# Sums from transposed quarters, shorter runs of sums on GpSimd, and moments by twos in a fused attention and SwiGLU kernel

## The chip, the cores and the metric

The kernel runs on one core of a Trainium2 chip. The metric is device time in microseconds (us) of one execution; the time of a kernel is the median of its runs. The engines are called as the profile calls them: PE is TensorE (matmuls, transposes), ACT is ScalarE, DVE is VectorE, POOL is GpSimd, and SP is SyncE, which here only issues transfers. An engine works through its own queue in order; a transfer that POOL issues stands in POOL's queue between its sums.

## The reference

The input x has 2048 rows of 1024 values. Its rows are normalised, and the result goes through two branches whose outputs are combined:

```python
xn = _layernorm(x)                          # (x - mean) / sqrt(var + 1e-5), by row
# A: linear attention, 32 heads of 32
qkv = xn @ wqkv                             # 1024 -> 3 x 1024
phi = lambda t: where(t > 0, t + 1, exp(t)) + 1e-6
kv  = einsum("bhsd,bhse->bhde", phi(k), v)  # summed over all 2048 rows
z   = phi(k) summed over the rows
s   = (phi(q) @ kv) / (phi(q) . z + 1e-6) @ wo
# B: SwiGLU with 3584 hidden columns
out = (silu(xn @ w1) * (xn @ w3)) @ w2
return x + s * silu(out)
```

All values are float32.

## The kernel before

**Arithmetic.** Every large product is cut into two by two blocks and done with seven block products instead of eight (the Winograd form of Strassen's method). On the left it needs the quarters A11, A12, A22 of the rows and four sums of quarters:

S1 = A21 + A22, S2 = S1 - A11, S3 = A11 - A21, S4 = A12 - S2.

The right-hand side has its own four sums, T1 to T4. Each operand is split (`split`, L79) into a rounded high part, which ACT writes (L83), and the rest, which DVE writes (L84); a block product takes three matmuls for each slice of 128 (`mm3`, L89 to L94).

**Halves.** The rows are taken in two halves of 1024 (`half`, L426), each as two chunks of 512. A half needs its seven operands (`AOPS`) transposed, with the 1024 columns of x on the partitions: 128 partitions, high and low part, 4 slices, 512 rows. With these it makes keys and values, then queries, then the gate and up products (`gemm`, L310: keys and values of 4 pairs, queries of 4 pairs, gate and up of 14 pairs). The second stage, attention and the down product (`Segment`, L715), follows the two halves.

**First half's operands.** `prepare_first` (L158) loads four tiles of 128 rows, takes each one's mean and 1/sqrt(variance) (`moments`, L124), normalises it (L145), and turns A11 and A12 with four PE transposes each (L152). `prepare_rest` (L171) does the same for the four tiles of the second chunk, makes S1 to S4 on POOL (`combined`, L183, lines 186 to 189) from row tiles, and turns five operands. The order of these pieces among the first products is written out by hand at L450.

**Second half's operands.** `prepare_next` (L192) makes them while the first half's queries and first gate and up products run. Each of its four jobs loads two row tiles, takes moments of both, normalises them, makes the four sums on POOL with `combined`, turns seven operands (`turn`, L195; transposes at L198), splits each out of PSUM, and stores it in device memory (`a_d`, L201), from where the second half loads it.

**Fillers.** A job is a Python generator. `catch_up` (L298) is called six times in each product of `gemm` and takes the next step of the first job waiting; `issue_after` keeps the step's instructions behind the marks given. In the first half the jobs are the four of `prepare_next`, then 28 of `weight_sums` (L545), which load a piece of w2, make T1 to T4 on POOL (`sums_of`, L538, lines 540 to 543) and store them. In the second half they are `denominators` (L603), `merge_wo` (L657, which calls `sums_of` too) and `divide` (L631, which calls `four_sums`).

**Hidden tiles.** `hidden` (L514) takes a gate product through Silu on ACT into a tile `sg`, multiplies it by the up product on DVE (L524), stores it from POOL's queue (L525), and, once two tiles of a chunk are there, makes S1 to S4 on POOL (`four_sums`, L503, lines 509 to 512) into two tiles `hs`, which SP's queue stores (L534; POOL's for the last pair). `sg` has four buffers.

**Order.** The program is written in Python order. A planner (`schedule_with_timeline_sim`) then fixes each engine's order from its own estimates of when things are ready, and the order of the operations in the profile isn't always that of the text: sums of different steps stand side by side in POOL's queue. [...]

Of the kernel before, what the change touches and what calls it, by code (L numbers as in the profile page):

```python
# [9 lines left out]
F32 = mybir.dt.float32  # L10
# [12 lines left out]
def tile_linear_attention_times_swiglu(  # L23
# [100 lines left out]
    def moments(xs, dst):  # L124

        n = len(xs)
        bs = st.tile([P, n, 2, nc.vector.BN_STATS_DIM], F32, tag="bs", name="bs")
        v = st.tile([P, n], F32, tag="v", name="v")
        u = st.tile([P, n], F32, tag="u", name="u")
# [4 lines left out]
        y = dst[:, :, 1]  # L134
        nc.vector.tensor_scalar_add(v, y, 1e-5)
# [4 lines left out]
        nc.vector.tensor_mul(u, u, v)  # L140
        nc.vector.tensor_scalar(u, u, -0.5, 1.5, op0=ALU.mult, op1=ALU.add)
        nc.vector.tensor_mul(y, y, u)
# [27 lines left out]

    def prepare_rest(A, mom, i, t0):  # L171

        t1 = job_tile([P, D], f"xb{i}") if i < 3 else pb.tile([P, D], F32, tag="b", name=f"xb{i}")
        nc.sync.dma_start(out=t1, in_=x[C + i * P:C + (i + 1) * P, :])
        j = TH // 2 + i
        moments([t1], mom[:, j:j + 1])
        normalise(t1, mom[:, j])
# [14 lines left out]
    def prepare_next(i):  # L192


        def turn(n, src):  # L195
            p_ = bank(f"t{n}1_{i}")
            for k in range(ND // 2):
                nc.tensor.transpose(p_[:, k * P:(k + 1) * P], src[:, k * P:(k + 1) * P], ident)  # L198
            o = pb.tile([P, 2, ND // 2, P], FR, tag="b", name=f"{n}o{i}")
            split(o, p_.rearrange("p (k s) -> p k s", k=ND // 2))  # L200
            nc.sync.dma_start(out=a_d[n][:, :, :, i * P:(i + 1) * P], in_=o.bitcast(F32))  # L201

        def steps(_):
            t0, t1, t2 = (job_tile([P, D], f"xn{i}_{e}") for e in range(3))
            for c, t in enumerate((t0, t1)):
                r0 = HS + c * C + i * P
                nc.sync.dma_start(out=t, in_=x[r0:r0 + P, :])
# [3 lines left out]
            moments([t0, t1], m)  # L211
            yield True
            yield True
            normalise(t0, m[:, 0])
            yield True
            normalise(t1, m[:, 1])
# [731 lines left out]
```

## Time and profile before

| | us |
|---|---|
| median of 3 runs | 2450.59 (2450.36 to 2451.07) |
| the profiled execution | 2447.93 |
| its span, first to last instruction | 2446.1 |
| PE busy | 2358.0 (96%) |
| DVE busy | 1792.1 (73%) |
| ACT busy | 919.8 (38%) |
| POOL busy | 724.4 (30%) |
| mean granted clock of PE | 0.992 |

Busy time is the time in which an engine has an instruction under way, and this includes the time in which an instruction under way is held up by something else. A row of a timeline gives start and duration in us, engine, line, operation, the tile written and the tiles read, their shapes, and how many equal instructions it stands for. A row of a wait gives who waited for whom, the total, how often, and the longest. The stages lie about so in the span: the first half's operands until 64 us, its keys and values to about 200, its queries to about 320, its gate and up products to about 890, the second half to about 1740, then attention's output and the down product.

### The profile page before, as it was taken

Reading aid. Unit: us, or ns where it says so; the run is one execution under the profiler, and the core shown is the slowest. Engines: PE = TensorE matmul, PEld = TensorE weight load, DVE = VectorE, ACT = ScalarE, POOL = GpSimd, SP = SyncE. Lnnn points to the kernel's source line nnn. Section 1 sums busy time; section 2 is a strip of 40 time slices with the busy share of each in tenths; the row PEclk is TensorE's granted clock in tenths of the full one; section 3 lists DMA queues with packets and bytes.
Section 4 is the critical chain, followed back from the end, with each engine's and each line's share of the span. In section 5 each row is a group of like instructions: output and inputs, shape, how many; then the busy total and the mean of one; then the engine's idle time right before and its main releaser. Section 6 shows DMA issues by size and latency. Waiting matters only on the chain.

```text
span 2446.1 us, 31065 instructions
## 1 busy us (share of the span) xinstructions
PE 2358.0 (96%) x10624; PEld 1941.1 (79%) x10624; DVE 1792.1 (73%) x2694; ACT 919.8 (38%) x1648; POOL 724.4 (30%) x873
## 2 busy tenths in 40 slices
PE   5999998999999999999999999999999999999998
PEld 4788887778888888888888888888787788787876
DVE  7654777797777765558878878887745776767798
ACT  4333543323333234445433233323423434343443
POOL 3000122264545310001235552354210032323244
PEclk9999999999999999999999999999999999999999
DMA  3112455575656491124355664566755554454588
GB/s 129 52 52 69 140 170 162 157 257 181 207 173 219 149 345 52 35 78 153 128 196 200 218 227 151 183 230 216 241 157 178 149 156 143 134 153 127 161 277 266
DMA packets 377423, 408.12 MB, mean 167 GB/s; under 512 B 19824, under 2 KB 307568, under 8 KB 377264
## 3 DMA queue, kind: packets, MB, share of 16 engines
q1 hardware_dynamic: 355248, 332.46, 43.2%
q0 software_dynamic: 22016, 73.68, 8.0%
q8 instruction: 83, 1.36, 0.2%
q14 instruction: 76, 0.62, 0.1%
HBM read 268.44 MB, written 137.63 MB: 166 GB/s over the span
## 4 chain that ended last, share of the span: by engine, by line
PE 79%; DVE 11%; issue 4%; DMA 4%; ACT 2%; POOL 1%; SPq 0%; DVEq 0%; ACTq 0%; POOLq 0%
PE dB L92 1%; PE dB L94 1%; PE cB L92 1%; PE dB L93 1%; PE cB L94 1%; PE cB L93 1%; PE kv L415 1%; PE aB L94 1%; PE aB L92 1%; PE aB L93 1%; DMA wpr<-wp_d 1%; DVE acc L865 1%; PE trk L382 1%; DMA rT2B<-wt_d 1%; DMA rA11B<-h_d 1%
## 5 line engine op out<-in xcount | busy, mean ns | idle before, releaser
L474 POOL DMA_DIRECT2D pq_d<-pq x32 | 17.5, 547 | 502.0 <-DVE pq L376 501.9
L525 POOL DMA_DIRECT2D h_d<-sg x112 | 61.5, 549 | 278.5 <-DVE sg L524 257.8
L792 POOL TENSOR_TENSOR acc<-acc,uB 128x512 f32<-128x512 f32 x25 | 41.9, 1676 | 158.4 <-DVE uB L790 158.4
L540 POOL TENSOR_TENSOR w<-w 128x256 f32<-128x256 f32 x28 | 27.8, 992 | 103.5 <-DMA w<-in_B_w 103.5
L509 POOL TENSOR_TENSOR qd<-qd 128x128 f32<-128x128 f32 x32 | 26.6, 832 | 104.2 <-DVE qd L650 100.6
L512 POOL TENSOR_TENSOR hs<-sg,hs 128x256 f32<-128x256 f32 x56 | 54.9, 981 | 2.1
L771 POOL TENSOR_TENSOR acc<-acc,uB 128x512 f32<-128x512 f32 x7 | 11.7, 1666 | 145.8 <-ACT uB L763 145.8
L856 POOL DMA_DIRECT2D s_d<-s x32 | 17.3, 540 | 122.5 <-DVE s L798 64.5
L383 ACT ACTIVATE kvr<-trk 128x512 f32<-128x512 f32 x32 | 19.1, 597 | 77.7 <-PE trk L382 77.5
L510 POOL TENSOR_TENSOR hs<-hs,sg 128x256 f32<-128x256 f32 x56 | 45.9, 820 | 0.0
L511 POOL TENSOR_TENSOR hs<-sg 128x256 f32<-128x256 f32 x56 | 42.8, 765 | 0.0
L509 POOL TENSOR_TENSOR hs<-sg,sg 128x256 f32<-128x256 f32 x56 | 42.0, 749 | 1.1
L92 PE MATMUL cB<-T,XA22B 128*128 128x512 f32 x87 | 35.0, 403 | 6.6 <-DVE acc L796 6.2
L794 POOL TENSOR_TENSOR acc<-acc,uB 128x512 f32<-128x512 f32 x25 | 40.1, 1604 | 0.0
L83 ACT CAST XS4B<-rS4B 128x384 fp32r<-128x384 f32 (+1 forms) x40 | 19.6, 490 | 53.2 <-PE cB L94 45.2
L807 DVE TENSOR_TENSOR acc<-cB,acc 128x512 f32<-128x512 f32 x25 | 17.2, 688 | 30.2 <-PE cB L94 30.2
L84 DVE TENSOR_TENSOR XS1B<-rS1B,XS1B 128x384 fp32r<-128x384 f32 (+1 forms) x40 | 37.2, 931 | 1.7 <-ACT XS1B L83 1.6
L863 ACT ACTIVATE acc<-acc 128x512 f32<-128x512 f32 x32 | 20.2, 632 | 47.2 <-DVE acc L798 14.1
L83 ACT CAST XA11B<-rA11B 128x384 fp32r<-128x384 f32 (+1 forms) x40 | 19.7, 493 | 45.8 <-PE dB L94 28.4
L83 ACT CAST XS1B<-rS1B 128x384 fp32r<-128x384 f32 (+1 forms) x40 | 19.7, 493 | 45.4 <-PE cB L94 26.5
L83 ACT CAST XS3B<-rS3B 128x384 fp32r<-128x384 f32 (+1 forms) x40 | 19.6, 491 | 43.7 <-PE bB L94 15.6
L92 PE MATMUL aB<-B,XA12B 128*128 128x512 f32 x87 | 34.1, 392 | 1.9 <-ACT uB L788 1.6
(5864 smaller groups left out, 8907.8 us busy)
## 6 DMA issues: line engine op xcount, KB each, us to landing
h_d<-sg POOLq DMA_DIRECT2D x112, 256.0 KB, 4.4
hs_d<-hs SPq DMA_DIRECT2D x104, 256.0 KB
qs_d<-qd POOLq DMA_DIRECT2D x32, 512.0 KB, 4.4
w<-in_B_w SPq DMA_DIRECT2D x56, 256.0 KB
wt_d<-w SPq DMA_DIRECT2D x28, 512.0 KB
pq_d<-pq POOLq DMA_DIRECT2D x32, 256.0 KB, 3.0
pqd<-pq_d SPq DMA_DIRECT2D x16, 512.0 KB
S<-a_dS SPq DMA_DIRECT2D x16, 512.0 KB
```

What stands on the lines that cost most here:

```text
L83: nc.scalar.copy(out=hi, in_=src)
L84: nc.vector.tensor_sub(out=lo, in0=src, in1=hi.bitcast(F32))
L92: nc.tensor.matmul(acc, lhsT=wh, rhs=ah, start=start, stop=False, skip_group_check=True)
L93: nc.tensor.matmul(acc, lhsT=wh, rhs=al, start=False, stop=False, skip_group_check=True)
L94: nc.tensor.matmul(acc, lhsT=wl, rhs=ah, start=False, stop=stop, skip_group_check=True)
L509: nc.gpsimd.tensor_add(out=s1, in0=a21, in1=a22)
L510: nc.gpsimd.tensor_sub(out=s2, in0=s1, in1=a11)
L511: nc.gpsimd.tensor_sub(out=s3, in0=a11, in1=a21)
L512: nc.gpsimd.tensor_sub(out=s4, in0=a12, in1=s2)
L525: nc.gpsimd.dma_start(out=h_d[i][2 * h + c][:, 2 * k + n], in_=sg[n, c])
L792: G.tensor_add(out=c22, in0=c22, in1=u)
L794: G.tensor_add(out=c12, in0=c12, in1=u)
```

## The change

**`moments`** takes up to two tiles at once, and its last steps are fused: u = -0.5 y y v in one operation, and (u + 1.5) y in another, instead of a product, a scale and shift, and a product. `prepare_first` calls it for two tiles together, where it called it tile by tile. A new `load_second` loads the second chunk's tiles by twos and takes their moments together; `prepare_rest` calls it for tiles 0 and 2.

**`prepare_next`** turns the four quarters A11, A12, A21, A22 instead of the seven operands. A11 and A12 are split and stored out of PSUM as before, and ACT copies them, and A21, from PSUM over the row tile's own quarter. A22 is split and stored out of PSUM. The sums are then made on DVE, in place, from the transposed quarters, and split from there. It uses two job tiles instead of three.

**Runs of sums on POOL.** `four_sums` now yields after S1 and S2 and after S3 and S4; in `hidden` a store stands at each yield, and all these stores are issued from POOL's queue. `sums_of` yields, that is, ends a step, between its two pairs of sums; `weight_sums` begins its sums one step earlier, and `merge_wo` has one step more in each second job. `divide` runs through `four_sums` without anything between.

```diff
     def moments(xs, dst):
         n = len(xs)
-        bs = st.tile([P, n, 2, nc.vector.BN_STATS_DIM], F32, tag="bs", name="bs")
-        v = st.tile([P, n], F32, tag="v", name="v")
-        u = st.tile([P, n], F32, tag="u", name="u")
+        bs = st.tile([P, 2, 2, nc.vector.BN_STATS_DIM], F32, tag="bs", name="bs")
+        v, y, u = (st.tile([P, 2], F32, tag=a, name=a)[:, :n] for a in "vyu")
...
-        y = dst[:, :, 1]
-        nc.vector.tensor_scalar_add(v, y, 1e-5)
+        nc.vector.tensor_scalar_add(v, dst[:, :, 1], 1e-5)
         nc.scalar.activation(y, v, AF.Sqrt)
         nc.vector.reciprocal(y, y)
         nc.vector.tensor_mul(u, y, y)
-        nc.vector.tensor_mul(u, u, v)
-        nc.vector.tensor_scalar(u, u, -0.5, 1.5, op0=ALU.mult, op1=ALU.add)
-        nc.vector.tensor_mul(y, y, u)
+        nc.vector.scalar_tensor_tensor(u, u, -0.5, v, op0=ALU.mult, op1=ALU.mult)
+        nc.vector.scalar_tensor_tensor(dst[:, :, 1], u, 1.5, y, op0=ALU.add, op1=ALU.mult)
@@ prepare_first
-            for e in range(2):
-                i = 2 * g + e
-                xs.append(t[:, e])
-                moments(xs[i:], mom[:, i:i + 1])
+            xs += [t[:, e] for e in range(2)]
+            moments(xs[2 * g:], mom[:, 2 * g:2 * g + 2])
+            for i in (2 * g, 2 * g + 1):
                 normalise(xs[i], mom[:, i])
@@ prepare_rest
+    def load_second(mom, g):
+        ts = []
+        for i in (2 * g, 2 * g + 1):
+            ts.append(job_tile([P, D], f"xb{i}") if i < 3 else pb.tile([P, D], F32, tag="b", name=f"xb{i}"))
+            nc.sync.dma_start(out=ts[-1], in_=x[C + i * P:C + (i + 1) * P, :])
+        j = TH // 2 + 2 * g
+        moments(ts, mom[:, j:j + 2])
+        return ts
...
+        if i % 2 == 0:
+            seconds += load_second(mom, i // 2)
@@ prepare_next
+            return p_
+        def keep(n, src):
             o = pb.tile([P, 2, ND // 2, P], FR, tag="b", name=f"{n}o{i}")
-            split(o, p_.rearrange("p (k s) -> p k s", k=ND // 2))
+            split(o, src.rearrange("p (k s) -> p k s", k=ND // 2))
             nc.sync.dma_start(out=a_d[n][:, :, :, i * P:(i + 1) * P], in_=o.bitcast(F32))
...
-            turn("A11", t0[:, :C])
-            yield True
-            turn("A12", t0[:, C:])
-            yield True
-            b = combined(t0, t1, t2[:, :C])
-            yield True
-            for n in ("A22", "S1", "S3", "S2", "S4"):
-                yield True
-                turn(n, b[n])
+            for n, a in (("A11", a11), ("A12", a12)):
+                p_ = turn(n, a)
+                keep(n, p_)
+                nc.scalar.copy(out=a, in_=p_)
+                yield True
+            p_ = turn("A21", a21)
+            nc.scalar.copy(out=a21, in_=p_)
+            yield True
+            p_ = turn("A22", a22)
+            keep("A22", p_)
+            nc.vector.tensor_add(out=a22, in0=p_, in1=a21)
+            yield True
+            nc.vector.tensor_sub(out=a21, in0=a11, in1=a21)
+            keep("S1", a22)
+            yield True
+            keep("S3", a21)
+            nc.vector.tensor_sub(out=a11, in0=a22, in1=a11)
+            yield True
+            keep("S2", a11)
+            nc.vector.tensor_sub(out=a12, in0=a12, in1=a11)
+            yield True
+            keep("S4", a12)
             yield True
@@ four_sums
         nc.gpsimd.tensor_sub(out=s2, in0=s1, in1=a11)
+        yield
         nc.gpsimd.tensor_sub(out=s3, in0=a11, in1=a21)
         nc.gpsimd.tensor_sub(out=s4, in0=a12, in1=s2)
+        yield
@@ hidden, sums
-            four_sums(sg[0, c], sg[1, c], *o)
-            for e in range(2):
-                queue = nc.gpsimd if pair == NF // 2 - 1 else nc.sync
-                queue.dma_start(out=hs_d[i][2 * h + c][:, k, e], in_=o[e])
+            for e, _ in enumerate(four_sums(sg[0, c], sg[1, c], *o)):
+                nc.gpsimd.dma_start(out=hs_d[i][2 * h + c][:, k, e], in_=o[e])
@@ sums_of
         nc.gpsimd.tensor_sub(out=b12, in0=b22, in1=b12)
+        yield True
         nc.gpsimd.tensor_sub(out=b22, in0=b22, in1=b11)
@@ weight_sums
             yield True
-            yield True
-            sums_of(*(t[:, i] for i in range(4)))
+            yield from sums_of(*(t[:, i] for i in range(4)))
             yield True
@@ divide
-            four_sums(t[:, 0], t[:, 1], t[:, 2], t[:, 3])
+            for _ in four_sums(t[:, 0], t[:, 1], t[:, 2], t[:, 3]):
+                pass
@@ merge_wo
-                sums_of(*b)
+                yield from sums_of(*b)
```

More of the change, by code (lines that the diff above doesn't have):

```diff
@@ L169, in prepare_first, with prepare_rest @@
         return xs
[L171 to L177, printed above, removed]
+    def load_second(mom, g):
[6 more added lines that the diff above has]
+        return ts
+    def prepare_rest(A, mom, i, t0, seconds):
+        if i % 2 == 0:
+            seconds += load_second(mom, i // 2)
+        t1 = seconds[i]
+        normalise(t1, mom[:, TH // 2 + i])
         b = combined(t0, t1, small(f"S1x{i}"))
@@ L198, in turn @@
                 nc.tensor.transpose(p_[:, k * P:(k + 1) * P], src[:, k * P:(k + 1) * P], ident)
+            return p_
+        def keep(n, src):
             o = pb.tile([P, 2, ND // 2, P], FR, tag="b", name=f"{n}o{i}")
-            split(o, p_.rearrange("p (k s) -> p k s", k=ND // 2))
+            split(o, src.rearrange("p (k s) -> p k s", k=ND // 2))
             nc.sync.dma_start(out=a_d[n][:, :, :, i * P:(i + 1) * P], in_=o.bitcast(F32))
         def steps(_):
-            t0, t1, t2 = (job_tile([P, D], f"xn{i}_{e}") for e in range(3))
-            for c, t in enumerate((t0, t1)):
+            t = [job_tile([P, D], f"xn{i}_{e}") for e in range(2)]
+            for c in range(2):
                 r0 = HS + c * C + i * P
-                nc.sync.dma_start(out=t, in_=x[r0:r0 + P, :])
+                nc.sync.dma_start(out=t[c], in_=x[r0:r0 + P, :])
             for _ in range(3):
@@ L445, in half @@
             mom = st.tile([P, TH, 2], F32, tag="mom", bufs=1, name="mom")
-            xs = prepare_first(A, mom)
+            xs, seconds = prepare_first(A, mom), []
             m = [keys(0, early=True), values(0, early=True), keys(1, early=True)]
-            r = [prepare_rest(A, mom, i, xs[i]) for i in range(TH // 2)]
+            r = [prepare_rest(A, mom, i, xs[i], seconds) for i in range(TH // 2)]
             for kind, i in zip("mrrrmmrmrmrmrr", (0, 0, 1, 2, 1, 0, 3, 2, 0, 1, 1, 2, 2, 3)):
```

7 lines of the change are left out of this document (4 added, 3 removed).

## The prediction

> **What bounds the kernel now.** I read the page's head first, then the table of stretches, then who TensorE (PE) waited for, then the timeline around each of its longest waits.
>
> ```profile
> PE 2358.0 (96%) x10624; PEld 1941.1 (79%) x10624; DVE 1792.1 (73%) x2694; ACT 919.8 (38%) x1648; POOL 724.4 (30%) x873
> ```
>
> PE is the bound, idle for 4% of the span. So a change can gain in two ways: fewer PE instructions, or fewer of those idle stretches (and of the half-speed clock behind them). The stretches (columns: length, then PE, PEld, DVE, ACT, POOL busy, clock, DMA share, GB/s) say where they lie:
>
> ```profile
> 279.00:560.00 281.00, 263.60 (x1176) 214.52 (x1175) 221.05 (x306) 105.56 (x182) 98.95 (x120) 0.97 0.59 185
> 600.00:800.00 200.00, 200.00 (x884) 165.67 (x883) 153.65 (x190) 62.45 (x105) 102.62 (x124) 1.00 0.58 196
> ```
>
> From 600 to 800 us PE is never idle: nothing that VectorE (DVE) or GpSimd (POOL) saves there can count. From 279 to 560 us, where the second half's operands are prepared, PE is idle for 281 - 263.6 = 17.4 us and its clock is at 0.97, another 281 x 0.03 = 8.4 us. Its waits (us in total, times, longest), at the start and from 380 to 520 us:
>
> ```profile
> PE tA L152 <- DVE xa L145: 21.8, 3, 12.3
> PE bk__696 L92 <- ACT T2k__682 L83: 8.0, 1, 8.0
> ```
>
> ```profile
> PE ag__4061 L94 <- DVE B21g__4050 L84: 5.2, 1, 5.2
> PE ag__3357 L94 <- DVE B11g__3331 L84: 3.8, 1, 3.8
> PE bg__3380 L92 <- ACT T2g__3339 L83: 2.7, 1, 2.7
> PE bu__3890 L92 <- ACT T2u__3854 L83: 1.8, 1, 1.8
> ```
>
> 29.8 us are the start; 5.2 + 3.8 + 2.7 + 1.8 = 13.5 us are four waits for weight splits. The timeline (start, duration) shows why two of them were late:
>
> ```profile
> 396.78 4.88 DVE L84 TENSOR_TENSOR B11g__3331<-wg__3329,B11g__3331 128x512 fp32r<-128x512 f32 x1
> ...
> 500.42 10.28 DVE L84 TENSOR_TENSOR B21g__4050<-wg__4033,B21g__4050 128x512 fp32r<-128x512 f32 x1
> ```
>
> ```profile
> 399.18 1.25 POOL L189 TENSOR_TENSOR xn<-xn 128x512 f32<-128x512 f32 x1
> 400.40 0.71 POOL L512 TENSOR_TENSOR hs<-sg,hs 128x256 f32<-128x256 f32 x1
> ...
> 508.75 1.39 POOL L543 TENSOR_TENSOR w<-w 128x256 f32<-128x256 f32 x2
> ```
>
> Below, such an operation takes 0.68 us. Here it ends about 0.6 us after the last sum of an unbroken POOL run: at 401.7 after a run that ends at 401.1, at 510.7 after one that ends at 510.1. So while POOL sums run back to back, a DVE operation on two SBUF tiles is held to the end of the run. DVE runs in order, so each later split is late too.
>
> **The change, part by part.** The sum is made against the profiled execution, 2447.93 us (1.8 us around its span); the median of the runs is 2450.59, which is 2.66 more.
>
> *Transposes.* Each of four preparations turns four 128x512 quarters instead of seven operands: 12 turns, 48 transposes, go.
>
> ```profile
> 413.65 0.39 PE L94 MATMUL dg__3382<-S,T1g__3335 128*128 128x512 f32 x1
> 413.88 0.60 PE L198 MATMUL tA<-ident,xn 128*128 128x128 f32 x4
> 414.31 0.27 PE L198 MATMUL tS<-ident,xn 128*128 128x128 f32 x1
> 414.34 0.47 PE L94 MATMUL bg__3380<-S,T2g__3339 128*128 128x512 f32 x1
> 414.65 0.39 PE L92 MATMUL bg__3380<-S,T2g__3339 128*128 128x512 f32 x1
> ```
>
> Five transposes took 414.34 - 413.88 = 0.46 us, 0.092 each; the matmul behind them took 0.31 to its successor instead of 0.23. A turn thus costs 4 x 0.092 + 0.08 = 0.45 us on the bounding engine. 12 x 0.45 = **-5.4 us** (-4.4 without the switch, -6.5 if it is paid on both sides).
>
> *Preparing the second half.* The sixteen POOL sums go; DVE gets sixteen, ACT twelve copies of turned quarters out of PSUM.
>
> ```profile
> L189 POOL TENSOR_TENSOR xn<-xn x4: 1250/1295/1687, 283.8 to 467.2; 128x512 f32<-128x512 f32 x4
> ...
> L83 ACT CAST S4o<-tS x4: 580/587/599, 306.6 to 501.6; 128x512 fp32r<-128x512 f32 x4
> L84 DVE TENSOR_TENSOR S4o<-tS,S4o x4: 678/680/681, 307.7 to 511.8; 128x512 fp32r<-128x512 f32 x4
> ```
>
> The columns are ns: least, median, most. POOL loses 16 x 1.3 = 21 us of runs, DVE gains 16 x 0.68 = 11 us, ACT 12 x 0.59 = 7 us. ACT is busy 105.56 of 281 us and hides its part. DVE is busy 221.05 of 281, part of it being held. Against the change stands that S4o above, read from PSUM, was never held, while its successor reads two SBUF tiles: 16 splits and 12 of the sums become liable to be held. What falls away: POOL's runs shrink here by the L189 kind, and what stays (hidden sums, weight sums) is cut into twos by a store or a step. How much a cut helps shows at 1731 us, where a store of sums already stands between sums:
>
> ```profile
> 1730.50 3.28 DVE L84 TENSOR_TENSOR wp<-wpr,wp 128x512 fp32r<-128x512 f32 x2
> ```
>
> ```profile
> 1732.12 0.73 POOL L511 TENSOR_TENSOR hs<-sg 128x256 f32<-128x256 f32 x1
> 1732.79 0.56 POOL L534 DMA_DIRECT2D hs_d<-hs  x1
> 1733.37 1.00 POOL L510 TENSOR_TENSOR hs<-hs,sg 128x256 f32<-128x256 f32 x1
> ```
>
> The first of the two DVE operations takes its 0.6, so the held one gets about 2.7 us, ends at 1733.78 and has been let in at the store, although two more sums follow. A hold of 2.7 instead of 4.9 to 10.3 us is nearer to the 600 to 800 us stretch, where PE doesn't wait at all. Best case: all 13.5 us of those waits and 8 us of clock behind them go, -21.5. Worst: none goes and the new DVE work lies wholly on the path, +11. The row nearest to the case is the cut run, so I take -21.5 and give back 4.5 for the 28 operations newly liable and the sums that wait, in DVE's order, for a turn on PE: **-17 us**. Next late is what makes up the other 17.4 - 13.5 = 3.9 us, which stays.
>
> [...]
>
> *Moments by twos.* At the start six small operations for each tile become five for two tiles, and the chain from statistics to normalise loses one link.
>
> ```profile
> 20.61 0.20 DVE L141 TENSOR_SCALAR u<-u 128x1 f32<-128x1 f32 x2
> ...
> 23.23 0.21 DVE L142 TENSOR_TENSOR mom<-mom,u 128x1 f32<-128x1 f32 x2
> ```
>
> Between links lie 23.23 - 20.61 = 2.6 us of other DVE work, and PE's first waits are for the normalise at the chain's end. One link less: **-2.4 us**. If another link is also overtaken less, -5; if the first tile's normalise waits for the second's statistics with nothing regained, +3. The second four tiles, loaded by twos, have PE's products as cover, which begin with this row:
>
> ```profile
> 29.19 0.79 PE L92 MATMUL ak__341<-A,B11k__334 128*128 128x512 f32 x1
> ```
>
> *Stores on POOL's queue, steps.* 104 stores of hidden sums leave SP's queue.
>
> ```profile
> L534 SPq DMA_DIRECT2D hs_d<-hs x104: 319/336/2637, 360.7 to 1691.0; - x104
> ...
> L534 POOL DMA_DIRECT2D hs_d<-hs x8: 539/557/559, 884.9 to 1736.0; - x8
> ```
>
> POOL pays 104 x 0.557 = 58 us, at 30% busy over the whole span; behind a store only the next pair of sums waits. SP stops waiting for sums ahead of weight fetches. The weight sums come a step earlier, so POOL may wait longer for their load, with stores of sg tiles behind it:
>
> ```profile
>   ACT sg L521: 9.2, 4
> ```
>
> ACT waited 9.2 us behind such sums and PE not at all. **0**, from -1 to +6 (two thirds of that wait reaching PE).
>
> [...]
>
> *Second half of the run.* Where wo is merged, PE waits as well:
>
> ```profile
> PE cg__9630 L92 <- DVE c22g__9657 L344: 1.4, 1, 1.4
> PE wp L92 <- ACT kvm L83: 1.4, 1, 1.4
> ```
>
> The merged sums are cut too, one step longer in each of four jobs. I take **-2** (-2.8, or +2 if the longer jobs crowd the end).
>
> Sum: -5.4 - 17 - 2.4 + 0 - 2 = -26.8. 2447.93 - 26.8 = 2421.1 for a profiled execution, 2423.8 on the median: **2424 us**.
>
> **The rivals.**
>
> *Holds replaced by other waits.* The planner may still line up sums of different steps (the run that ends at 401.1 us already mixes an xn sum with hidden sums), and the new DVE sums come in ahead of weight splits. For it: DVE is busy 0.79 of this stretch; against it: stores now stand between the sums. Then the transposes, the start and a third of -21.5 remain against a few us of new waits: 2450.6 - 5.4 - 2.4 - 7 + 4 = 2440. This is also what follows if breaking the runs doesn't do what it says.
>
> *One instruction at a time.* If a held operation waits for a single sum, runs don't matter and cutting gains nothing: only the 1.25 us that L189 put into one wait, the 1.8 us wait behind its longest row (1687 ns), 8.4 / 4 = 2.1 us of clock behind that one, transposes and start: 2450.6 - 3.05 - 2.1 - 5.4 - 2.4 = 2438. Against it: the 10.28 row. [...]
>
> *Slower.* DVE now waits in order for a chain PE, ACT, DVE in each preparation. ACT waited for such turns before:
>
> ```profile
>   ACT A22o L83: 11.4, 3
> ```
>
> That is 3.8 us each. Eight such waits (A21 and A22 of four preparations) would be 30 us of DVE standing before weight splits. Its place is DVE's queue, and it decides once a wait comes between a split and the product that needs it within about a microsecond, as at 397 us. With half of it on PE and 2.1 us of clock behind each of four, 15 + 8 us, and the old waits unmended: 2450.6 + 23 - 7.8 = 2466. Against it: the planner put ACT's and DVE's work on S1o to S4o behind the same kind of turns without a wait of PE of that size.
>
> **How the numbers follow.** Forecast 0.62 (its own range 2411 to 2437, from the terms' ends taken partly together); replaced waits 0.19; one at a time 0.05; slower 0.09; no change, small terms of both signs, 0.05. A difference under 0.2% (4.9 us) can't be told from none here. Faster: 0.62 + 0.19 + 0.05 less a little of the second, 0.84; same 0.06; slower 0.10. The range leaves out the last two and reaches over the first rivals: 2411 to 2445.
>
> **What would show it.** 48 fewer instructions of PE; no POOL sum of xn after 100 us; the first product before 29 us; from 280 to 560 us DVE operations of at most 3 us and PE idle for under 9 us at a clock of 0.99. The forecast is wrong if PE's idle time there stays near 17 us, or if new waits of more than 3 us for DVE's sums or ACT's copies appear.

## The result, and the profile after

The changed kernel takes **2516.23 us** (2508.32 to 2518.87), against 2450.48 for the kernel before beside it: a ratio of **1.0264, 95% interval 1.0239 to 1.0289**. It is 65 us slower, where 27 us faster was forecast; the time lies far outside the range, and the forecast's rival on the slower side (2466) doesn't reach it either. The profiled execution took 2518.11 us.

The head of the page after, and the group that stands out in its list (busy time and mean, then the idle time of the engine just before the group, and what ended it):

```profile
span 2516.3 us, 30839 instructions
...
PE 2379.0 (95%) x10576; PEld 1950.9 (78%) x10576; DVE 1805.1 (72%) x2678; ACT 925.9 (37%) x1656; POOL 761.0 (30%) x961
...
L673 DVE SCALAR_TENSOR_TENSOR qd<-qd 128x512 f32<-128x512 f32 x32 | 23.1, 721 | 87.0 <-DMA qd<-pq_d 87.0
```

PE has 48 instructions fewer and is nevertheless busy for 21 us longer, and its idle time has grown as well. The group below it belongs to a part of the kernel that the change hardly touches: L673 is the VectorE product in `divide` (L650 before, where `divide` begins at L633; lines behind `prepare_next` are 23 to 25 higher than before). DVE stood 87 us in front of it, for its loads. In the kernel before, the same group has 0.0 us of idle time in front of it (21.8 us busy, 682 ns each).

The stretches say where the time went (columns as in the prediction). Before:

```profile
1300.00:1800.00 500.00, 495.92 (x2174) 406.98 (x2173) 397.47 (x519) 170.99 (x292) 212.40 (x316) 1.00 0.62 206
```

After:

```profile
279.00:560.00 281.00, 262.30 (x1158) 212.75 (x1157) 229.02 (x328) 117.12 (x199) 97.07 (x130) 0.98 0.60 193
1300.00:1800.00 500.00, 450.22 (x1881) 363.71 (x1880) 358.60 (x456) 146.76 (x253) 223.67 (x336) 0.95 0.53 177
```

In the last stretch PE is idle 495.92 - 450.22 = 45.7 us more, and its clock falls from 1.00 to 0.95, another 500 x 0.05 = 25 us. Added, these are about 71 us, an estimate, since the clock is given to two places; the two profiled executions lie 70.2 us apart, so the loss lies in this stretch in the main. The stretch from 279 to 560 us, on which the forecast rested, has stayed as it was: PE idle for 281 - 262.30 = 18.7 us (17.4 before), clock 0.98 (0.97 before). Who waited, in the whole run (total, times, longest):

```profile
DVE qd L673 <- DMA qd<-pq_d: 87.0, 16, 8.3
PE cg__12885 L92 <- DVE c22g__12917 L367: 9.1, 1, 9.1
PE bg__2990 L92 <- ACT T2g__2954 L83: 6.1, 1, 6.1
PE cg__13211 L92 <- DVE c22g__13243 L367: 5.9, 1, 5.9
PE cg__11221 L92 <- DVE c22g__11253 L367: 5.4, 1, 5.4
PE ak__321 L93 <- DVE A L84: 4.0, 1, 4.0
```

Three of the PE waits are one kind: PE adds its next block product to PSUM bank c, and L367, which has to read the bank first, is late. From 1300 to 1800 us such waits for L367 make up 37.7 us. The timeline around a smaller one shows why (start, duration; the bracket is the idle time before):

```profile
PE cu__11050 L92 <- DVE c22u__11082 L367: 3.2, 1, 3.2
```

```profile
1387.04 0.69 DVE L673 SCALAR_TENSOR_TENSOR qd<-qd 128x512 f32<-128x512 f32 x1 [6.86 <-DMA qd<-pq_d]
1391.18 0.68 DVE L673 SCALAR_TENSOR_TENSOR qd<-qd 128x512 f32<-128x512 f32 x1
...
1396.18 0.57 POOL L676 DMA_DIRECT2D qs_d<-qd  x1 [0.30 <-POOL qd L536]
...
1400.72 0.38 SPq L261 DMA_DIRECT2D wu__11172<-in_B_w  x1
1401.21 0.54 SPq L665 DMA_DIRECT2D qd<-r_d  x1
...
1403.89 1.94 SPq L667 DMA_DIRECT2D qd<-pq_d  x1
...
1412.23 0.69 DVE L673 SCALAR_TENSOR_TENSOR qd<-qd 128x512 f32<-128x512 f32 x1 [7.57 <-DMA qd<-pq_d]
1412.84 0.68 DVE L367 TENSOR_TENSOR c22u__11082<-cu__11050,uu__11028 128x512 f32<-128x512 f32 x1
...
1438.01 0.69 DVE L673 SCALAR_TENSOR_TENSOR qd<-qd 128x512 f32<-128x512 f32 x1 [7.23 <-DMA qd<-pq_d]
```

DVE stands for 7.57 us in front of a division, and L367, the sum that reads the bank, stands right behind it: PE's last matmul into the bank ahead of that sum ran from 1404.33 to 1404.72, and L367 began at 1412.84, 0.61 us after the division. ACT and POOL show the same order of work in the kernel before: ACT stood 2.48 us, until 500.53, for a weight piece, with the S4 that it copied at 501.58 turned by 496.05; POOL stood 1.37 us, until 489.24, for a load, with the hidden tiles that it stored from 489.92 on done by 487.23.

So the question was: why are the loads of a division late now, when the work of `divide` and its loads are as before?

### The profile page after: what moved, and what is told of

The parts are those of the page before. It is cut to its first block, busy times and chain, and to the rows that moved or that the text cites. A ratio compares the mean times of both kernels' runs of the same rounds, so it can differ in the third digit from the quotient of the medians.

```text
span 2516.3 us, 30839 instructions
## 1 busy us (share of the span) xinstructions
PE 2379.0 (95%) x10576; PEld 1950.9 (78%) x10576; DVE 1805.1 (72%) x2678; ACT 925.9 (37%) x1656; POOL 761.0 (30%) x961
## 4 chain that ended last, share of the span: by engine, by line
PE 54%; DMA 11%; DVE 7%; issue 4%; POOL 2%; SPq 2%; ACT 1%; DVEq 0%; POOLq 0%; ACTq 0%
DMA qd<-pq_d 4%; DMA qs_d<-qd 2%; PE dB L92 1%; PE dB L94 1%; PE dB L93 1%; PE cB L92 1%; PE cB L94 1%; PE cB L93 1%; PE aB L94 1%; PE aB L92 1%; PE aB L93 1%; SPq L665 1%; DMA wpr<-wp_d 1%; SPq L667 1%; DMA rS1B<-hs_d 1%
## 5 line engine op out<-in xcount | busy, mean ns | idle before, releaser
L497 POOL DMA_DIRECT2D pq_d<-pq x32 | 17.4, 545 | 520.4 <-DVE pq L399 498.4
L673 DVE SCALAR_TENSOR_TENSOR qd<-qd 128x512 f32<-128x512 f32 x32 | 23.1, 721 | 87.0 <-DMA qd<-pq_d 87.0
L557 POOL DMA_DIRECT2D hs_d<-hs x112 | 62.0, 554 | 5.9 <-POOL hs L536 3.3
L563 POOL TENSOR_TENSOR w<-w 128x256 f32<-128x256 f32 x28 | 25.8, 922 | 94.9 <-DMA w<-in_B_w 94.8
L533 POOL TENSOR_TENSOR hs<-hs,sg 128x256 f32<-128x256 f32 x56 | 51.4, 917 | 0.1
L535 POOL TENSOR_TENSOR hs<-sg 128x256 f32<-128x256 f32 x56 | 43.5, 776 | 0.0
```

The costliest lines, as they stand in the source:

```text
L533: nc.gpsimd.tensor_sub(out=s2, in0=s1, in1=a11)
L535: nc.gpsimd.tensor_sub(out=s3, in0=a11, in1=a21)
L557: nc.gpsimd.dma_start(out=hs_d[i][2 * h + c][:, k, e], in_=o[e])
```

## The experiments

All ratios are to the kernel before on the same chip, with 95% intervals. Job k is the k-th of the 32 divisions, counted from 0. A step is what a job does up to its next yield, and a mark is an instruction that `issue_after` keeps a step behind.

### First round: which part of the change is it?

**e1, the merged sums of wo in one step.** The changed kernel, with the one step more taken away: 181 steps stand ahead of the divisions again, instead of 185.

```diff
-                yield from sums_of(*b)
+                for _ in sums_of(*b):
+                    pass
```

> The changed kernel, but merge_wo makes its four sums in one step again, so that the second half's jobs have 181 steps as before and not 185. Theory 'rhythm': four more steps shift the three-step divide jobs against the six steps of a product, so that divide's DVE product (which waits for a late load) comes ahead of the sum that empties a PSUM bank, and PE waits behind it. Then this kernel loses nothing in the second half: 2445 to 2452 us. Rival 'stores': the 104 stores of hidden sums in POOL's queue delay the qs stores, and with them the loads into the job tiles. Then it stays at 2505 to 2518 us.

Measured: 2451.98 us, 1.0020 (1.0009 to 1.0031). Of 65 us, 60 hang on this one `yield`.

**e2, stores of hidden sums on SP's queue as before.**

```diff
-                nc.gpsimd.dma_start(out=hs_d[i][2 * h + c][:, k, e], in_=o[e])
+                queue = nc.gpsimd if pair == NF // 2 - 1 else nc.sync
+                queue.dma_start(out=hs_d[i][2 * h + c][:, k, e], in_=o[e])
```

> The changed kernel, but with the stores of hidden sums issued from SP's queue as before. Rhythm: the divide jobs stand where they stand in the changed kernel, 2500 to 2518 us. Stores: the loads come in time again, 2445 to 2455 us.

Measured: 2524.98 us, 1.0313 (1.0294 to 1.0332). The stores aren't it.

**e3, the kernel before with one empty step more** in each second job of `merge_wo`; no work is added.

```diff
-                for _ in range(3):
+                for _ in range(4):
```

> The kernel before with nothing but one more empty step at the end of each second merge_wo job (four steps in all). Rhythm: this alone brings the loss of the second half, 2490 to 2520 us. Stores: an empty step does nothing, 2449 to 2453 us.

Measured: 2521.72 us, 1.0299 (1.0279 to 1.0319). Four empty steps alone cost the kernel before 73 us, with the same wait as in the changed kernel:

```profile
DVE qd L650 <- DMA qd<-pq_d: 83.4, 13, 10.7
```

**e4, the cut kept, the steps as before.** The changed kernel with `range(2)` there: the sums are cut, and 181 steps stand ahead.

```diff
-                for _ in range(3):
+                for _ in range(2):
```

> The changed kernel with merge_wo's sums still cut by a step, and one empty step less at its end, so 181 steps in all. Rhythm: it is the count of steps and not the cut, 2445 to 2452 us, like the kernel with whole sums. Stores: 2505 to 2518 us. If the cut of merge_wo's sums itself did the harm, also 2505 to 2518 us.

Measured: 2453.57 us, 1.0024 (1.0014 to 1.0033). So it is not the cut that costs, but something in the number of steps.

**e5, a fourth job buffer** in the changed kernel (with `kvm` moved to another pool to make room).

```diff
-        return praw.tile(shape, F32, tag="job", bufs=3, name=name)
+        return praw.tile(shape, F32, tag="job", bufs=4, name=name)
```

> The changed kernel with four job tiles instead of three (kvm of merge_wo lies in a pb tile to make room); all 185 steps stay. Theory 'late load': DVE's product in divide waits because the load into its tile is issued only when the store out of the same tile, three jobs back, has landed; with a fourth tile the load is issued earlier, DVE's waits for qd fall from 87 us to under 20 and the time to 2445 to 2465 us. Rival 'place': the product's place ahead of the sum that empties the bank costs by itself, whatever the load does: 2495 to 2518 us.

Measured: 2527.78 us, 1.0324 (1.0311 to 1.0337); DVE waits as before.

```profile
DVE qd L673 <- DMA qd<-pq_d: 88.1, 15, 10.2
```

The theory that too few buffers make the loads late fell, as it then stood.

### Second round: the parts alone, on the kernel before

**e6, the quarters alone** (the new `prepare_next`); **e7, the moments alone**; **e8, the cut runs alone** (stores of hidden sums on POOL's queue between the pairs of sums, `sums_of` cut in `weight_sums`, but whole in `merge_wo`). Their diffs are those parts of the change.

> The kernel before with prepare_next of the changed one alone (four turns, sums on DVE from transposed quarters). Forecast's theory: 48 transposes fewer and the held splits gone, 22 us less, 2421 to 2432 us. Rival 'replaced waits': eight or so DVE operations of the preparation now stand in a row ahead of the weight splits, and PE waits for T2 as long as it waited before; only the transposes remain, about 5 us less, 2438 to 2445 us.

> The kernel before with moments by twos alone. Forecast's theory: first product about 2 us earlier and all behind it too, 2443 to 2446 us. Rival 'normalise in a row': all four xb tiles are normalised in a row ahead of the last splits of A, PE waits 4 us there and runs at half speed behind it: 3 to 6 us more, 2449 to 2454 us.

> The kernel before with the cut runs on POOL alone: stores of hidden sums from POOL's queue between the pairs of sums, weight sums cut by a step and begun a step earlier; merge_wo's sums stay whole, so the second half's steps count as before. Forecast's theory: holds of DVE are shorter, PE's waits behind the 4.9 and 10.3 us holds go: 2425 to 2438 us. [...]

Measured: e6 2450.26 us, 1.0008 (0.9999 to 1.0016); e7 2457.88 us, 1.0043 (1.0030 to 1.0057); e8 2451.64 us, 1.0009 (1.0001 to 1.0018). No part brings anything by itself, and the moments cost 10 us.

**e12, quarters and cut runs together**, moments as before, wo's sums in one step.

> The quarters and the cut runs of sums together, with the moments as before and the merged sums of wo in one step (181 steps). Theory (the parts add up; the one with all parts but the step cost 1.0020, moments alone 1.0043): 2440 to 2448 us, ratio 0.996 to 0.999. Rival (the moments cost nothing once the runs are cut, the quarters give nothing): 1.000 to 1.003 like the others.

Measured: 2449.0 us, 1.0001 (0.9992 to 1.0011): the rival. Together they bring nothing either.

### Third round: the number of steps, its remainder, or the place

A gate or up product has six places for a step and a division takes three steps, so two divisions fall to each product, and the remainder by three of the steps ahead of them decides at which places their products stand.

**e9, three of the four jobs longer:** 184 steps, the remainder of 181.

```diff
-                for _ in range(3):
+                for _ in range(4 if k < 3 else 3):
```

> The kernel before, with one empty step more in three of the four second jobs where wo is merged: 184 steps instead of 181 stand before the divisions. Theory (the divisions take three steps and a product has six places for a step, so only the remainder by three decides where each division falls): the division's VectorE product comes back to its two old places, no wait of VectorE for qd, 2450 us (ratio 0.999 to 1.003). Rival (more steps ahead make the work late, whatever the remainder): three quarters of the four-step loss, about 2505 us. PE from 1400 to 1600 us is busy over 198 by the theory, under 190 by the rival.

Measured: 2451.76 us, 1.0018 (1.0008 to 1.0027). The number itself costs nearly nothing.

**e10, two of the four longer:** 183 steps, the third remainder.

```diff
-                for _ in range(3):
+                for _ in range(4 if k < 2 else 3):
```

> The kernel before, with one empty step more in two of the four second jobs: 183 steps, remainder zero by three, a third place that no kernel so far had (the division's VectorE product between c22's second part and c21, and between u and c22). Theory A (only a place right ahead of a bank's emptying with a late load is dear): half of the divisions stand in the dear place between u and c22, so 2480 to 2530 us. Theory B (only the exact mixture of the changed kernel is dear): 2450 to 2460 us. Rival (steps in all count): about 2485 us, half of the four-step loss, with waits spread over the stretch rather than at the qd product.

Measured: 2447.48 us, 0.9999 (0.9989 to 1.0008). My theory A fell: here all 32 products stand at the two places (behind c22's second part, and between u and c22) where 28 of the changed kernel's stand, and it costs nothing.

**e11, the changed kernel with four buffers and each load issued a job earlier.**

```diff
-        data = [j.load() for j in work[:2]]
+        data = [j.load() for j in work[:3]]
...
-            if i + 2 < len(work):
-                data.append(work[i + 2].load())
+            if i + 3 < len(work):
+                data.append(work[i + 3].load())
```

> The changed kernel with four job buffers instead of three and each job's load issued three jobs ahead instead of two; places of the divisions stay those of the changed kernel. Theory (the division waits because its small loads are issued behind a 1 MB weight fetch on the same queue, and come too late): VectorE's waits for qd fall from 87 us to under 15, and the time to 2450 to 2470 us. Rival (the place itself is dear, load or not, through POOL's sums and VectorE's order): the time stays at 2505 to 2530 us, PE's waits for c22 move to another releaser.

Measured: 2531.06 us, 1.0336 (1.0318 to 1.0353), and DVE waits for qd as long as before. Asking for the loads a job earlier doesn't help; what their place behind a weight fetch costs, e11 doesn't separate (the last section has a row on it).

```profile
DVE qd L673 <- DMA qd<-pq_d: 84.9, 15, 9.9
```

### What the slow kernels have in common

The trace leaves the jobs' numbers out of the name `qd`, but the built kernels hold them. This is the order of the 32 divisions' products in DVE's queue:

```
before, e1, e4, e6 to e10, e12:   0 1 2 3 4 5 6 7 8 9 10 11 12 ...
after, e2, e3:                    0 2 4 1 6 3 8 5 10 7 12 9 14 11 13 15 16 18 20 17 22 19 ...
e5, e11 (four buffers):           0 2 4 6 1 8 3 10 5 12 7 14 9 11 13 15 16 18 20 22 17 19 ...
```

Every slow kernel so far has the jobs out of order, every other one has them in order. With this the timeline above can be read anew. Its products are those of jobs 8, 5, 10 and, at 1438.01, 12. When job 10's load is issued at 1401.21, two of the three `job` buffers are taken by jobs 7 and 9, whose products come later; the third was freed by the store of job 5 at 1396.18, and job 5's product stands on DVE *behind* that of job 8. So every even job is a link of one closed chain:

- product of job 8, 1387.04, and of job 5 behind it, 1391.18;
- POOL's four sums and the store's issue, 5.0 us later, 1396.18;
- the store lands, and SP issues job 10's loads, 5.0 us later, 1401.21 to 1405.83;
- they land, 6.4 us later, and job 10's product begins at 1412.23.

That is 25.2 us for a round, and 25.8 to the next at 1438.01. Without waits PE does a round, two divisions, in half of the time between two of these rows of the kernel before, which show every fourth of its divisions:

```profile
1351.10 0.68 DVE L650 SCALAR_TENSOR_TENSOR qd<-qd 128x512 f32<-128x512 f32 x1
...
1389.17 0.68 DVE L650 SCALAR_TENSOR_TENSOR qd<-qd 128x512 f32<-128x512 f32 x1
...
1427.25 0.68 DVE L650 SCALAR_TENSOR_TENSOR qd<-qd 128x512 f32<-128x512 f32 x1
```

38.08 / 2 = 19.04 us. In order, job 10 would have reused the buffer of job 7, three divisions or 28.6 us before it; out of order the way from job 5's product to job 10's has less than one round of 19.04, and the round then takes 25. PE pays the difference: by the products of jobs 4, 14, 18 and 30 in the changed kernel,

```profile
1339.07 0.69 DVE L673 SCALAR_TENSOR_TENSOR qd<-qd 128x512 f32<-128x512 f32 x1 [6.37 <-DMA qd<-pq_d]
...
1464.00 0.69 DVE L673 SCALAR_TENSOR_TENSOR qd<-qd 128x512 f32<-128x512 f32 x1 [8.28 <-DMA qd<-pq_d]
...
1591.28 0.69 DVE L673 SCALAR_TENSOR_TENSOR qd<-qd 128x512 f32<-128x512 f32 x1 [7.55 <-DMA qd<-pq_d]
...
1736.28 0.69 DVE L673 SCALAR_TENSOR_TENSOR qd<-qd 128x512 f32<-128x512 f32 x1 [5.70 <-DMA qd<-pq_d]
```

five rounds take 124.9 us, 29.7 more than 5 x 19.04, and six take 145.0, 30.8 more. That a fourth buffer doesn't help follows from the third row of the list: the even jobs have moved one further ahead. The built kernels also say whose buffer a job takes over. In the changed kernel job 10 takes that of job 5, in e5 and in e11 that of job 3, and in both orders this is the job whose product stands just ahead of its own; in the kernel before it takes that of job 7, three products ahead. The order and the buffers of e11 are those of e5, so asking for the loads earlier left the chain as it was.

Behind the order I suspected the marks. `issue_after` ties a step only to marks of the same engine. Five of the six places of a product have a DVE sum among their marks; the first, behind the first block product, has only ACT's copy. With 185 steps every second division falls on that place, and the planner is then free to put its product anywhere on DVE. A mark keeps a step behind something and sets no limit on how late it comes, so this was a suspicion and no proof.

### Fourth round: the order

**e13, the products kept in order.** The changed kernel, 185 steps, loads and buffers unchanged.

```diff
-            nc.vector.scalar_tensor_tensor(t[:, :2], t[:, :2], 1e-6, t[:, 2:], op0=ALU.add, op1=ALU.mult)
+            with ExitStack() as behind:
+                for d in divided[-1:]:
+                    behind.enter_context(tc.issue_after(d.ins))
+                divided.append(nc.vector.scalar_tensor_tensor(
+                    t[:, :2], t[:, :2], 1e-6, t[:, 2:], op0=ALU.add, op1=ALU.mult))
```

> The changed kernel; each division's VectorE product is put behind the previous division's on VectorE's queue, so that the jobs' products stand in order 0, 1, 2, 3 instead of 0, 2, 4, 1, 6, 3. Step count, loads and buffers are unchanged. Theory (the inverted order makes every second job pass through one buffer, so that a division's load must wait for the store of the division just before it): 2450 to 2460 us (ratio 1.001 to 1.004), VectorE's waits for qd under 15 us instead of 87. Rival (the place of the division behind c22's second part, or the longer work, is what costs): 2505 to 2530 us, for now 31 of 32 products stand there.

Measured: 2457.37 us, 1.0032 (1.0021 to 1.0043). Now 31 of the 32 stand between c22's second part and c21, as the rival had it, and yet 57 us are gone; DVE's wait has shrunk to a fifth (the 15 us expected were just missed).

```profile
DVE qd L678 <- DMA qd<-pq_d: 16.2, 7, 3.3
```

**e15, the kernel before with one DVE mark taken away**, at the sixth place; steps and work unchanged.

```diff
-        catch_up(copied, added)
+        catch_up(copied)
```

> The kernel before, with the step behind c21's sum tied to ScalarE's copy alone and no longer to a VectorE operation (as the first step of each product is in both kernels). Steps and all work are unchanged; the planner then puts the divisions in order 1, 0, 3, 2, 5, 7, 4, 9, 6, 11. Theory (inverted order is the cause): slower, 2480 to 2530 us (ratio 1.012 to 1.032), with waits of VectorE for qd of 30 us or more. Rival (the step count or the place is the cause): 2447 to 2455 us.

Measured: 2521.6 us, 1.0301 (1.0286 to 1.0317). The products stand in the order 1 0 3 2 5 7 4 9 6 11 8, and the wait is there, in a kernel that has nothing of the change:

```profile
DVE qd L650 <- DMA qd<-pq_d: 105.8, 15, 10.2
```

**e16, the changed kernel with a DVE mark for the first place:** the last sum (c12) of the product before.

```diff
-        nc.vector.tensor_add(out=c12, in0=bd, in1=u)
+        ended[:] = [nc.vector.tensor_add(out=c12, in0=bd, in1=u)]
...
-        catch_up(copied)
+        catch_up(copied, *ended)
```

> The changed kernel; only the first step of each product is tied to the last VectorE sum of the product before it (c12), as the other steps are tied to a VectorE sum. The divisions come back into order 0, 1, 2, 3, at the places that 185 steps give them (between c22's second part and c21, and behind c12). Theory: 2450 to 2460 us (ratio 1.001 to 1.004). Rival (place or length): 2505 to 2530 us. It is the smallest mend of the change.

Measured: 2454.79 us, 1.0030 (1.0020 to 1.0039). The order is 0, 1, 2, 3 at 185 steps, a single wait of DVE for qd of 1.2 us is left of the 87, and the last stretch is nearly back to what it was:

```profile
1300.00:1800.00 500.00, 492.72 (x2135) 401.61 (x2134) 395.80 (x514) 168.38 (x291) 229.84 (x354) 0.99 0.62 204
```

The cause is thus shown from both sides: taking a mark away from the kernel before turns the order round and makes it slow, giving one to the changed kernel, or fixing the order alone (e13), makes it fast again. What remains open is why the planner, once free, puts these products later and not earlier.

### Fifth round: the moments

In e7 PE's first product starts earlier, as forecast, but then stands. Its timeline at the start:

```profile
27.17 4.86 DVE L142 TENSOR_SCALAR xb<-xb,mom 128x1024 f32<-128x1024 f32 x4
...
27.43 0.60 PE L92 MATMUL ak__321<-A,B11k__314 128*128 128x512 f32 x1
...
32.68 0.80 PE L93 MATMUL ak__321<-A,B11k__314 128*128 128x512 f32 x1 [4.19 <-DVE A L84]
...
33.70 0.63 PE L92 MATMUL ak__321<-A,B11k__314 128*128 128x512 f32 x1
34.13 0.63 PE L93 MATMUL ak__321<-A,B11k__314 128*128 128x512 f32 x1
...
38.41 0.40 PE L93 MATMUL av__402<-A,B11v__395 128*128 128x512 f32 x1
38.65 0.39 PE L94 MATMUL av__402<-A,B11v__395 128*128 128x512 f32 x1
```

The second four tiles, whose statistics now come in pairs, are normalised all four in a row, ahead of the splits of A that the first product needs. PE stands 4.19 us, and its matmuls follow each other at 0.43 us until about 38, and at 0.24 after. The granted clock from 25 to 45 us is 0.83, where the kernel before has 1.00. The changed kernel has the same wait, 3.96 us long, and behind it a clock of 0.50 from 33 to 38 us.

**e17, e7 with the second four tiles one by one** as before, in the shorter chain.

```diff
-        if i % 2 == 0:
-            seconds += load_second(mom, i // 2)
-        t1 = seconds[i]
+        t1 = job_tile([P, D], f"xb{i}") if i < 3 else pb.tile([P, D], F32, tag="b", name=f"xb{i}")
+        nc.sync.dma_start(out=t1, in_=x[C + i * P:C + (i + 1) * P, :])
+        j = TH // 2 + i
+        moments([t1], mom[:, j:j + 1])
```

> The moments alone as in e7, but the second four tiles loaded, measured and normalised one by one as before (with the shorter chain). Theory (the loss comes from the four xb tiles that are normalised in a row, 4.86 us ahead of the splits that PE waits for): the gain at the first product stays, 2443 to 2449 us (ratio 0.998 to 1.000). Rival (the loss comes from pairing the first four tiles or from the shorter chain itself): 2455 to 2460 us as in e7 (1.0043).

Measured: 2453.58 us, 1.0024 (1.0014 to 1.0033): between the two, so neither theory nor rival held. By the two ratios the pairing was 0.0019 of 0.0043, nearly half of the loss, but their intervals (1.0030 to 1.0057 and 1.0014 to 1.0033) just meet. The largest part of the rest lies at 360 us, where e7 has a wait that e17 has too, as long, and that is 1.2 us in the kernel before:

```profile
PE bg__2998 L92 <- ACT T2g__2957 L83: 8.0, 1, 8.0
```

```profile
364.06 0.56 POOL L530 DMA_DIRECT2D h_d<-sg  x1 [2.05 <-DVE sg L529]
364.29 3.66 DVE L262 TENSOR_TENSOR wg__2947<-wg__2947 128x512 f32<-128x512 f32 x1
364.64 0.73 POOL L517 TENSOR_TENSOR hs<-sg,hs 128x256 f32<-128x256 f32 x1
...
367.87 1.21 DVE L84 TENSOR_TENSOR T1g__2953<-wg__2947,T1g__2953 128x512 fp32r<-128x512 f32 x1
...
369.68 0.67 DVE L262 TENSOR_TENSOR wg__2947<-wg__2947 128x512 f32<-128x512 f32 x1
```

A subtraction on the weight tile is held by POOL's run for 3.66 us (the one at 369.68 took 0.67), and behind it in DVE's queue stand the split of T1 (367.87) and the subtraction that ACT needs for T2 (369.68). In the kernel before, a run of POOL at this place held the split of T3, which is needed later:

```profile
361.73 3.71 DVE L84 TENSOR_TENSOR T3g__3001<-wg__2987,T3g__3001 128x512 fp32r<-128x512 f32 x1
```

Behind a hold of the same 3.7 us PE didn't wait there; here it stands in the chain of a wait of 8.0 us, of which it explains some 3 us. An earlier subtraction on the same tile is held too (360.48, 2.08 us instead of 0.68), and the rest was not taken apart. That the shorter chain is what shifted the queues there was not tried by itself.

**e18, the changed kernel with e16's mark and the second four tiles one by one; e19, with the mark and the moments wholly as before.**

> The changed kernel with the mark of e16 and with the second four tiles loaded, measured and normalised one by one, with the shorter chain. If the costs of the parts add (the pairing of the second four cost 0.0043 - 0.0024 = 0.0019 alone): 1.0030 - 0.0019 = 1.0011, about 2450.5 us. Rival (the cost of the moments is swallowed by the other waits once quarters stand beside them): 2453 to 2457 us as in e16.

> The changed kernel with the mark of e16 and the moments wholly as before: quarters, stores, cut runs and the cut merged sums of wo at 185 steps. If the parts add (moments 0.0043): 1.0030 - 0.0043 = 0.9987, about 2444.7 us, faster than the kernel before. Rival (quarters and cut runs together gave 1.0001 without the cut of wo, so nothing is left to gain): 2446 to 2451 us, ratio 0.9995 to 1.0015.

Measured: e18 2450.71 us, 1.0004 (0.9994 to 1.0014); e19 2450.81 us, 1.0004 (0.9993 to 1.0015). Both are as fast as the kernel before and none is faster. In e18 the costs added as expected (1.0011 lies in the interval); in e19 the rival held.

## Why the prediction was wrong, point by point

**The step that failed: "Second half of the run".** "The merged sums are cut too, one step longer in each of four jobs. I take -2 (-2.8, or +2 if the longer jobs crowd the end)." What a longer job does to the work *behind* it was not asked. Four more steps move every division by one place of the six; every second one then falls on the place without a DVE mark; the planner puts these behind later ones; and a buffer that had three divisions' time to come round has less than two. By the pair after and e16 that cost 1.0264 - 1.0030 = 0.0234, **57 us**; in e3, on the kernel before, 73. The text of `catch_up`, with its marks, stood in the kernel before, so the free place could have been seen. That the planner would use it to turn the order round could not be read from the profile before. But a moved step moves every job behind it, and this could have had a rival of its own.

**The rival on the slower side** was the wrong mechanism: it had DVE's waits in `prepare_next`. Its pattern, DVE standing in order ahead of something that PE needs, was right, 900 us later.

**Transposes (-5.4) and preparing (-17).** Together -22.4 was forecast. The quarters alone (e6) show +2.0 us (0 to +4), and with the cut runs, which the -17 counted on, the two together (e12) +0.2 (-2 to +3). So the largest term failed too: it has its share in the missing gain, and none in the 57 us. The 48 instructions are gone (10576 against 10624), the first part of the reasoning held, and the holds have become shorter: the longest of 10.28 us has become

```profile
499.52 3.52 DVE L280 TENSOR_TENSOR wg__3960<-wg__3960 128x512 f32<-128x512 f32 x1
...
504.76 3.40 DVE L84 TENSOR_TENSOR B22g__3984<-wg__3960,B22g__3984 128x512 fp32r<-128x512 f32 x1
```

The first of them ends at 503.04, 0.6 us after the last sum of the run shown below, as the prediction's reading of such holds has it. But PE's idle time hasn't fallen, because other waits took their place: this was the rival "holds replaced by other waits", which had 0.19. The largest is the 6.1 us of bg__2990 above. DVE's queue just before it:

```profile
355.11 0.68 DVE L84 TENSOR_TENSOR A22o<-tA,A22o 128x512 fp32r<-128x512 f32 x1
...
361.71 0.68 DVE L84 TENSOR_TENSOR S2o<-xn,S2o 128x512 fp32r<-128x512 f32 x1
362.31 0.68 DVE L84 TENSOR_TENSOR B11g__2946<-wg__2944,B11g__2946 128x512 fp32r<-128x512 f32 x1
```

From the first of these rows to the second stand eight operations of the preparation (four splits, four sums), 0.60 us each, 4.8 in all, ahead of the weight split B11g and the chain to T2. Two subtractions of that chain are held by POOL besides (364.72, 2.40 us; 368.36, 2.55 us; the one before them, at 363.52, took 0.68), so both causes are in the 6.1 us, and they were not separated. The forecast gave back 4.5 us in all for such cases; this one wait is longer. That rival too was too kind: with quarters and cut runs together e12 shows 1.0001, where it had -10.6 us.

**"What stays (hidden sums, weight sums) is cut into twos by a store or a step"** held for the text and not for POOL's queue. The longer of the two holds above stood beside this run:

```profile
498.97 0.75 POOL L532 TENSOR_TENSOR hs<-sg,sg 128x256 f32<-128x256 f32 x1
499.67 0.75 POOL L535 TENSOR_TENSOR hs<-sg 128x256 f32<-128x256 f32 x1
500.36 0.74 POOL L567 TENSOR_TENSOR w<-w 128x256 f32<-128x256 f32 x1
...
501.75 0.73 POOL L533 TENSOR_TENSOR hs<-hs,sg 128x256 f32<-128x256 f32 x1
```

Five sums (one is left out here), three of a hidden tile and two of weight pieces, with no store between: S3 (L535) has moved ahead of the store that the text puts before it. The hold lasts to the end of the run, which speaks against the rival "one instruction at a time" as well.

**Moments (-2.4, bounds -5 to +3).** Measured 10 us slower (e7), outside the bounds. The gain at the first product is there (27.43 against 29.19 in the prediction's row). The sentence that failed is "The second four tiles, loaded by twos, have PE's products as cover": pairing them put 4.86 us of normalising between two matmuls of the first product. By e17 this is less than half of the loss; most of the rest is the wait at 360 us, whose cause stays open.

**Stores on POOL's queue, steps (0, from -1 to +6).** e8, which has the cut runs as well: +2.2 us (0 to 4), inside the bounds; e2 shows that in the changed kernel the stores gain nothing by going back to SP.

**What would show it:** of the five signs, three came true (48 fewer instructions, no sum of xn on POOL, the first product before 29 us) and two didn't: DVE operations of 3.5 us instead of at most 3, and PE idle for 18.7 us at 0.98 between 279 and 560 us instead of under 9 at 0.99. The last was named as the sign that the forecast is wrong, and it would have been even without the divisions: with the order mended, e16, e18 and e19 lie at 1.0030 to 1.0004.

## What to carry to other kernels

When a job gets longer, work out for every job behind it at which place it now runs, and look at what ties it to that place on *each* engine: a step without a mark on an engine is put there by the planner alone. Compare the order of the jobs in each engine's queue, not only their waits: a load that still comes late with one buffer more is a sign that jobs overtake each other, and here neither more buffers nor earlier loads helped. And before counting a stall as won, name what stands behind it in the same queue; here PE didn't wait behind one stall of 3.7 us, and an equally long one was part of a wait of 8 us.

## What the hardware showed beyond what was expected

The price of a late bank was paid twice here. From 1300 to 1800 us PE lost 45.7 us by standing and, by the estimate above, about 25 us by the lower clock (behind the 3.2 us wait of cu__11050 it is 0.50 from 1414 to 1416 us); in e16 most of both is gone (3.2 us more idle time than in the kernel before, clock 0.99).

On SP's queue a load of qd took 0.47 us to issue ahead of a weight fetch, in the kernel before,

```profile
1382.98 0.47 SPq L644 DMA_DIRECT2D qd<-pq_d  x1
1383.55 0.56 SPq L238 DMA_DIRECT2D wu__11281<-in_B_w  x1
```

and 1.94 us behind one, after (the row at 1403.89). It looked like the cause, but e13 and e16, which leave the text of the loads as it is and mend the order, are fast (1.0032 and 1.0030). In the closed chain it does lengthen the round: job 10's four loads take 4.6 us to issue, where the four ahead of the fetch take 2.2 (1398.46 to 1400.61), so some 2.4 of the 6.2 us that a round lasts beyond 19.04.
